# Attention decode with SwiGLU: the last V in W_Q's place, the first K ahead of the FFN weights, and spin matmuls in each pass

## The chip, the cores and the metric

One NeuronCore of a Trainium2 chip runs the kernel. The metric is the device time of one execution in microseconds (us). Engine names are those of the profile: PE is TensorE's matmul, PEld its weight load, DVE is VectorE, ACT ScalarE, POOL GpSimd, SP SyncE; SPq is SP's queue of DMA issues.

## What is computed

A decode step for four sequences. The input is normalised once, and the result is the input plus attention plus a gated FFN:

```python
xn = layernorm(x)                                    # x: (4, 1, 512)
q  = (xn @ wq)                                       # 32 heads of 128
k, v = the last 4096 of 16384 cached positions       # 8 K/V heads, each for 4 query heads
p  = softmax(q k^T / sqrt(128))
A  = (p v) @ wo
F  = (silu(xn @ w_gate) * (xn @ w_up)) @ w_down      # 512 -> 1792 -> 512
out = x + A + F
```

All of it is bf16. One K/V head with its four query heads is a group; K and V of a group are 4 MiB each for the four sequences. With eight groups, W_Q and W_O (4 MiB each) and three FFN matrices (1.75 MiB each), 81.0 MB come from HBM once each.

## The kernel before

**Tiles.** The 128 partitions hold 32 stretches of the window for each of the four sequences; a group's K and V are then 128 tiles of 128 x 128 (`KB` and `VB`, one buffer each, K loaded in two halves). A K tile is transposed on PE against the identity into PSUM (`transposes`, L371; eight tiles are a chunk, and three banks `ps_kt` take turns). A chunk is copied to SBUF (`KT`) by DVE (L301) or, for the five chunks of `ACT_CH`, by ACT (L250). `scores` (L384) multiplies the copied tile, as the stationary operand, by the 16 query columns of the group; a sequence's partitions thus also hold scores for the other sequences' queries.

**Softmax.** DVE takes maxima of the scores (L306, L308), PE transposes them (`maxima`, L391), and DVE builds from them a matrix of 16 x 16 (`CM`, L310 to L314) with which `shift` (L396, four matmuls of 512 columns) subtracts each query's maximum and masks the foreign sequences. ACT then takes the exponentials (L254) into `P`. `pv` has a matmul with ones for the denominators (L405) for every 16 tiles, and one matmul for each V tile (L407). `norm` on DVE (L318 to L325) divides and places the result for W_O.

**The order on PE.** The program begins with the Q projection (L351, 128 matmuls), then gate and up of the FFN (L358, 112 matmuls). Then a hardware loop of nine passes follows: pass r does transposes and scores of group r, then `pv` of group r - 1 (48 tiles, `maxima` of group r, the other 80), then `shift` of group r. `If` leaves out what a pass doesn't have: pass 0 has no `pv`, and pass 8 has only `down` (the FFN's last product, L417 and L421) and the last `pv`. Behind the loop a small permutation (L452) and the product with W_O (L460) add to the sum that `down` started in PSUM, and DVE and ACT copy the two halves of the result out.

**The order on DVE and ACT.** Before their loops, ACT computes the exponential of the FFN's gate (L246), and DVE finishes the gated product (L286 to L292), which `down` needs. Then come the groups, with `norm(r - 1)` behind `group(r)`.

**The order of the loads.** All large loads are issued by SP in one list: W_Q, gate, up, K0 (two halves), down, four of the 32 row blocks of W_O; then for each g from 1 to 7 the halves of K(g) and V(g - 1); then the last V in two halves, and the rest of W_O in two parts. A half of K waits until the same half of the group before is transposed (L210), V until `pv` of the group before is done (L215):

```python
def load_v(g):
    if g > 0:
        eng.wait_ge(s_pv, g + 1)
```

A wait in this list holds all that stands behind it.

Of the kernel before, what the change touches and what calls it, by code (L numbers as in the profile page):

```python
# [3 lines left out]
BF16 = mybir.dt.bfloat16  # L4
FP32 = mybir.dt.float32
ALU = mybir.AluOpType
# [4 lines left out]
def bass_parallel_sum__sliding_block_cached__swiglu_ffn__decode_kernel(  # L11
# [113 lines left out]
    d_v = sem("d_v")  # L125
    d_vh = sem("d_vh")
    s_const = sem("s_const")
# [36 lines left out]
    with nc.Block() as block:  # L164
# [39 lines left out]
        @block.sync  # L204
        def _(eng):
            H = NT // 2

            def load_k(g, h):
                if g > 0:
                    eng.wait_ge(s_tr, NCH * (g - 1) + (h + 1) * NCH // 2)  # L210
                eng.dma_start(KB[:, h * H:(h + 1) * H, :], kv_ap(A_k_cache, g, h * H, (h + 1) * H)).then_inc(d_k[h], 16)

            def load_v(g):
                if g > 0:
                    eng.wait_ge(s_pv, g + 1)  # L215
                for a, b, d in ((0, H, d_vh), (H, NT, d_v)) if g == HKV - 1 else ((0, NT, d_v),):
                    eng.dma_start(VB[:, a:b, :], kv_ap(A_v_cache, g, a, b)).then_inc(d, 16)  # L217
# [4 lines left out]
            eng.dma_start(WQ[:], wq_ap).then_inc(d_wq, 16)  # L222
# [12 lines left out]
            load_wo(2, WOB, NR)  # L235
            eng.wait_ge(s_y[0], 1)
            eng.dma_start(out_ap[0], y[0:B, :]).then_inc(d_out, 16)
            eng.wait_ge(d_out, 32)

        @block.scalar  # L240
        def _(eng):
            eng.dma_start(X[:], x_ap).then_inc(d_x, 16)
            eng.wait_ge(s_var, 1)
            eng.activation(st_std[:], st_var[:], ACT.Sqrt).then_inc(s_std, 1)
            eng.wait_ge(s_gu, 1)
            eng.activation(ex[:], gate_ps.rearrange("p (t b) -> p t b", b=B), ACT.Exp, scale=-1.0).then_inc(s_ex, 1)  # L246
            with eng.Fori(0, HKV) as r:
                for n, c in enumerate(ACT_CH):
                    eng.wait_ge(s_tr, r * NCH + (c + 1))
                    eng.activation(KT[:, c % 4], kt_ps[c % 3], ACT.Copy).then_inc(s_ea, 1)  # L250
                eng.wait_ge(s_pv, r + 1)
                for q in range(NB):
                    eng.wait_ge(s_mk, r * NB + (q + 1))
                    eng.activation(P[:, BT * q:BT * (q + 1), :], ps_S[q][:].rearrange("p (t n) -> p t n", n=NH),  # L254
                                   ACT.Exp, scale=SCALE).then_inc(s_p, 1)
            eng.wait_ge(s_acc, 1)
            eng.activation(y[64:64 + B, :], acc_ps[64:64 + B, 0:D // 2], ACT.Copy).then_inc(s_y[1], 1)  # L257
# [4 lines left out]
        def _(eng):  # L262
# [21 lines left out]
                            q_ps.rearrange("p (k h b) -> p k b h", k=HKV, b=B))  # L284
            eng.wait_ge(s_ex, 1)
            eng.tensor_scalar(ex[:], ex[:], 1.0, None, ALU.add)  # L286
            eng.drain()
            eng.reciprocal(ex[:], ex[:])
            eng.drain()
            eng.tensor_tensor(gs[:], gate_ps.rearrange("p (t b) -> p t b", b=B), ex[:], ALU.mult)  # L290
            eng.drain()
            eng.tensor_tensor(guT[:], up_ps.rearrange("p (t b) -> p t b", b=B), gs[:], ALU.mult).then_inc(s_guT, 1)  # L292

# [33 lines left out]

            group(0)
            with eng.Fori(1, HKV) as r:
                group(r)  # L330
                norm(r - 1)
# [7 lines left out]
        def _(eng):  # L339
# [13 lines left out]
            last.then_inc(s_q, 1)  # L353
            for w, d, o in ((WG, d_wg, gate_ps), (WU, d_wu, up_ps)):
                eng.wait_ge(d, 16)
                for t in range(NF):
                    for c in range(NC):
                        last = mm(o[:, t * B:(t + 1) * B],  # L358
                                  w[:].rearrange("p c (m t) -> p c t m", t=NF)[:, c, t, :], XnT[:, c, :],
                                  start=(w is WG and t == 0 and c == 0), stop=(c == NC - 1),  # L360
                                  skip_group_check=True)
            last.then_inc(s_gu, 1)
            eng.sem_inc(s_pv, 1)
# [35 lines left out]

            def pv(r, a, b):  # L400
                n = NT // DT
                for t in range(a, b):
                    if t % (NT // n) == 0:
                        e = t // (NT // n)
                        mm(den_ps, ones[:], P[:, DT * e:DT * (e + 1), :].rearrange("p t n -> p (t n)"),  # L405
                           start=(e == 0), stop=(e == n - 1), skip_group_check=True)
                    last = mm(O_ps, VB[:, t, :], P[:, t, :], start=False, stop=(t == NT - 1), skip_group_check=True)  # L407
                if b == NT:
                    last.then_inc(s_pv, 1)

            HD = D // 2
# [11 lines left out]

            with eng.Fori(0, HKV + 1) as r:
                with eng.If(r < HKV):
                    for c in range(NCH):
                        transposes(r, c)
                        if c >= 2:
                            scores(r, c - 2)
                    scores(r, NCH - 2)  # L430
                    scores(r, NCH - 1)
                with eng.If(r > HKV - 1):
                    down()
                    eng.wait_ge(d_vh, 16)
                with eng.If(r > 0):
                    eng.wait_ge(s_p, r * NB + NB)
                    eng.wait_ge(s_nrm, r)
                    with eng.If(r < HKV):
                        eng.wait_ge(d_v, r * 16)
                    pv(r, 0, 48)  # L440
                with eng.If(r < HKV):
                    maxima(r)
                with eng.If(r > 0):
                    pv(r, 48, NT // 2)
                    eng.wait_ge(d_v, r * 16)
                    pv(r, NT // 2, NT)
                with eng.If(r < HKV):
                    shift(r)

            eng.wait_ge(s_nrm, HKV + 1)  # L450
            for b in range(B):
# [3 lines left out]
            for q in range(3):  # L455
                eng.wait_ge(d_wo[q], 16)
                a, b = ((0, WOA), (WOA, WOB), (WOB, NR))[q]
                for e in range(a, b):
# [32 lines left out]
```

## Time and profile before

| | |
|---|---|
| time, median of 3 runs | 217.65 us (215.77 to 217.68) |
| the profiled execution: time, span | 217.74 us, 216.0 us |
| mean granted clock of PE | 0.826 |
| PE, PEld, DVE, ACT busy | 169.5, 147.8, 102.1, 60.8 us |
| HBM read, mean over the span | 81.01 MB, 375 GB/s |
| chain that ended last | DMA 60%, PE 31%, issue 4%, DVE 2% |

The span runs from the first to the last instruction of the profiled execution. The busy times are sums over the whole run; PE's includes the latency of each pipelined matmul, so it is not a measure of how full PE is. The chain is followed back from the last instruction to whatever released each step, so it tells which resource was waited for. The slices divide the span in forty equal parts of 5.4 us; `PEclk` in them is the clock granted to PE, in tenths of full speed, and a 5 is half clock.

### The profile page before, as it was taken

How to read it: one execution, taken by the hardware profiler on the slowest of the kernel's cores; microseconds unless marked ns; L12 is line 12 of the kernel's file. 1: busy time of each engine (PE TensorE's matmuls, PEld its weight loads, DVE VectorE, ACT ScalarE, POOL GpSimd, SP SyncE). 2: the span in 40 equal slices, each digit the busy share in tenths (PEclk: the TensorE clock that was granted, in tenths of full speed). 3: DMA queues.
4: the chain of work that ended last, by engine and by line, in shares of the span. 5: the costliest groups of instructions: out<-in, count | busy, mean ns of one | idle time of the engine just before them, and what ended most of it. 6: DMA issues, size and time to landing. Idle time of an engine off the chain costs nothing.

```text
span 216.0 us, 8057 instructions
## 1 busy us (share of the span) xinstructions
PE 169.5 (78%) x3520; PEld 147.8 (68%) x3520; DVE 102.1 (47%) x209; ACT 60.8 (28%) x77; POOL 5.8 (3%) x29
## 2 busy tenths in 40 slices
PE   0157689519979995998899699979959997974655
PEld 0157689508977994797779679977958896634533
DVE  5200058703863882388258636854961685300200
ACT  2200014205522550345055215605430551210000
POOL 8200000000000000000000000000000000000000
PEclk9999999955985997699679958997995899566557
DMA  7999999999898899999999999998999993099930
GB/s 280 400 416 431 427 421 393 394 473 397 326 394 303 349 419 434 394 397 428 422 413 479 391 434 437 434 431 367 425 407 431 455 407 152 12 425 419 454 150 1
DMA packets 4639, 81.12 MB, mean 376 GB/s; under 512 B 524, under 2 KB 536, under 8 KB 792
## 3 DMA queue, kind: packets, MB, share of 16 engines
q1 hardware_dynamic: 4616, 81.01, 89.3%
q8 instruction: 6, 0.10, 0.2%
q10 hardware_dynamic: 16, 0.01, 0.0%
q14 instruction: 1, 0.01, 0.0%
HBM read 81.01 MB, written 0.00 MB: 375 GB/s over the span
## 4 chain that ended last, share of the span: by engine, by line
DMA 60%; PE 31%; issue 4%; DVE 2%; SPq 1%; DVEq 0%
DMA vbuf<-in_A_v_cache_dram 39%; DMA kbuf<-in_A_k_cache_dram 12%; PE ps_o L407 11%; DMA wo_sb<-in_A_wo_dram 9%; PE ps_kt L371 8%; PE ps_o L405 6%; PE ps_kt L460 3%; PE ps_s L384 2%; DVE kT L301 1%; PE ps_s L396 1%; PE ps_kt L391 1%; DVE mx L306 1%; SPq L217 1%; SPq L224 0%; DVE y_sb L336 0%
## 5 line engine op out<-in xcount | busy, mean ns | idle before, releaser
L371 PE MATMUL ps_kt<-ident,kbuf 128*128 128x128 bf16 x1024 | 80.3, 227 | 1.3 <-DMA kbuf<-in_A_k_cache_dram 1.3
L371 PEld LDWEIGHTS ps_kt<-ident,kbuf 128*128 128x128 bf16 x1024 | 63.7, 102 | 4.9 <-issue 3.2
L301 DVE COPY kT<-ps_kt 128x1024 bf16<-128x1024 bf16 x88 | 57.5, 685 | 19.0 <-PE ps_kt L371 18.7
L250 ACT ACTIVATE kT<-ps_kt 128x1024 bf16<-128x1024 bf16 x40 | 41.0, 1024 | 35.4 <-PE ps_kt L371 35.4
L384 PE MATMUL ps_s<-qC,kT 128*128 128x16 bf16 x1024 | 44.9, 170 | 2.6 <-DVE kT L301 1.9
L384 PEld LDWEIGHTS ps_s<-qC,kT 128*128 128x128 bf16 x1024 | 37.4, 97 | 4.4 <-DVE kT L301 4.1
L407 PEld LDWEIGHTS ps_o<-p,vbuf 128*128 128x128 bf16 x1024 | 36.8, 105 | 3.2
L407 PE MATMUL ps_o<-p,vbuf 128*128 128x16 bf16 x1024 | 38.4, 175 | 0.0
L254 ACT ACTIVATE p<-ps_s 128x512 bf16<-128x512 f32 x32 | 16.5, 602 | 69.9 <-PE ps_s L396 69.9
L405 PE MATMUL ps_o<-p,ones 128*128 128x256 bf16 x64 | 22.6, 354 | 14.4 <-DMA vbuf<-in_A_v_cache_dram 13.6
L306 DVE TENSOR_REDUCE mx<-ps_s 128x16 f32<-128x512 f32 x32 | 22.1, 692 | 6.7 <-PE ps_s L384 3.6
L396 PE MATMUL ps_s<-cm,own 128*128 128x512 bf16 x32 | 14.4, 606 | 5.4 <-issue 5.4
L405 PEld LDWEIGHTS ps_o<-p,ones 128*128 128x128 bf16 x64 | 6.5, 102 | 16.4 <-issue 14.0
L318 DVE TENSOR_REDUCE den<-ps_o 128x16 f32<-128x256 f32 x8 | 3.4, 425 | 30.2 <-PE ps_o L407 30.2
L310 DVE TENSOR_TENSOR junk<-ps_kt,moff 16x128 f32<-16x128 bf16 x8 | 2.2, 279 | 17.8 <-PE ps_kt L391 17.8
L396 PEld LDWEIGHTS ps_s<-cm,own 128*128 128x128 bf16 x32 | 3.5, 128 | 9.9 <-issue 9.9
L460 PE MATMUL ps_kt<-wo_sb,oP 128*4 128x256 bf16 x64 | 7.1, 414 | 2.7 <-DMA wo_sb<-in_A_wo_dram 2.2
L460 PEld LDWEIGHTS ps_kt<-wo_sb,oP 128*4 128x4 bf16 x64 | 3.8, 122 | 5.7 <-DMA wo_sb<-in_A_wo_dram 2.7
L351 PE MATMUL ps_s<-xnT,wq_sb 128*128 128x4 bf16 x128 | 3.6, 166 | 5.1 <-DMA wq_sb<-in_A_wq_dram 5.1
L257 ACT ACTIVATE y_sb<-ps_kt 4x256 bf16<-4x256 f32 x1 | 0.4, 375 | 24.2 <-PE ps_kt L460 24.2
L351 PEld LDWEIGHTS ps_s<-xnT,wq_sb 128*128 128x128 bf16 x128 | 3.5, 104 | 5.2 <-issue 5.2
L344 PE MATMUL ps_s<-i,xn 4*128 4x4 f32 x4 | 0.6, 261 | 7.4 <-POOLq L202 7.4
(63 smaller groups left out, 52.5 us busy)
## 6 DMA issues: line engine op xcount, KB each, us to landing
kbuf<-in_A_k_cache_dram SPq DMA_DIRECT2D x16, 2048.0 KB, 12.3
vbuf<-in_A_v_cache_dram SPq DMA_DIRECT2D x7, 4096.0 KB, 14.2
wq_sb<-in_A_wq_dram SPq DMA_DIRECT2D x1, 4096.0 KB, 12.2
vbuf<-in_A_v_cache_dram SPq DMA_DIRECT2D x2, 2048.0 KB, 9.7
wo_sb<-in_A_wo_dram SPq DMA_DIRECT2D x1, 3328.0 KB, 19.3
wg_sb<-in_B_w_gate_dram SPq DMA_DIRECT2D x1, 1792.0 KB, 16.0
wu_sb<-in_B_w_up_dram SPq DMA_DIRECT2D x1, 1792.0 KB, 21.3
wd_sb<-in_B_w_down_dram SPq DMA_DIRECT2D x1, 1792.0 KB, 33.5
```

Source lines behind the costliest of these rows:

```text
L250: eng.activation(KT[:, c % 4], kt_ps[c % 3], ACT.Copy).then_inc(s_ea, 1)
L254: eng.activation(P[:, BT * q:BT * (q + 1), :], ps_S[q][:].rearrange("p (t n) -> p t n", n=NH), ACT.Exp, scale=SCALE).then_inc(s_p, 1)
L301: eng.tensor_copy(KT[:, c % 4], kt_ps[c % 3]).then_inc(s_ev, 1)
L306: eng.tensor_reduce(mx[:, q, :], ps_S[q][:].rearrange("p (t n) -> p n t", n=NH), AX.X, ALU.max)
L318: eng.tensor_reduce(den[:], den_ps.rearrange("p (t n) -> p n t", n=NH), AX.X, ALU.add)
L351: last = mm(q_ps[:, h * B:(h + 1) * B], WQ[:, c, h * Dh:(h + 1) * Dh], XnT[:, c, :], start=(c == 0 and h == 0), stop=(c == NC - 1), skip_g ...
L371: last = eng.transpose(kt_ps[c % 3][:, k, :], KB[:, CH * c + k, :], ident[:])
L384: last = mm(ps_S[q][:, NH * t:NH * (t + 1)], KT[:, c % 4, k, :], QC[:], start=(t == 0), stop=False, skip_group_check=True)
L396: mm(ps_S[q][:].rearrange("p (t n) -> p t n", n=NH), own[:], CM[:].unsqueeze(1).to_broadcast([128, BT, NH]), start=False, stop=True, skip_ ...
L405: mm(den_ps, ones[:], P[:, DT * e:DT * (e + 1), :].rearrange("p t n -> p (t n)"), start=(e == 0), stop=(e == n - 1), skip_group_check=True)
L407: last = mm(O_ps, VB[:, t, :], P[:, t, :], start=False, stop=(t == NT - 1), skip_group_check=True)
L460: last = mm(acc_ps[64 * n:64 * n + B, 0:HD], OP[:, e, :], WO[:, e, HD * n:HD * (n + 1)], start=False, stop=(e == NR - 1), skip_group_check ...
```

## The change

- **The last V.** The 4 MiB of W_Q are needed for the Q projection alone. The last V gets that place (`VL`, of which `WQ` is now a view), so its load waits only for the Q projection (`s_q`). It is in two halves with a semaphore each. `down` and the `pv` of the last group stand behind the loop on PE, which has eight passes.
- **The first loads.** K0 goes ahead of gate and up. The whole of W_O is loaded behind the last V, in parts of 16, 14 and 2 row blocks.
- **The FFN.** Gate and up are multiplied inside pass 0, behind `maxima`. ACT's exponential for it stands behind group 0's exponentials, and DVE's part behind `group(0)`.
- **Spin matmuls.** `spin` multiplies the matrix of ones by 512 columns into a bank `ps_kt` that is free at that point; nothing reads the result. A pass has three ahead of `maxima`, three behind it, and one inside `pv`; `pv` is no longer cut at 48 tiles for `maxima`.
- **Copies.** `ACT_CH` changes from (2, 5, 9, 11, 13) to (3, 5, 8, 10, 13).

```diff
-    ACT_CH = (2, 5, 9, 11, 13)
+    ACT_CH = (3, 5, 8, 10, 13)
-    WOA = 4
-    WOB = 30
+    WOS = (16, 30)
...
-    WQ = sb("wq_sb", [128, NC, HQ * Dh], BF16, 512)
+    VL = sb("vlast", [128, NT, Dh], BF16, 512)
+    WQ = VL[:].rearrange("p t d -> p (t d)").rearrange("p (c n) -> p c n", c=NC)
...
# SP
+            load_k(0, 0)
+            load_k(0, 1)
             eng.dma_start(WG[:], wg_ap).then_inc(d_wg, 16)
             eng.dma_start(WU[:], wu_ap).then_inc(d_wu, 16)
-            load_k(0, 0)
-            load_k(0, 1)
             eng.dma_start(WD[:], wd_ap).then_inc(d_wd, 16)
-            load_wo(0, 0, WOA)
             for g in range(1, HKV):
                 load_k(g, 0)
                 load_k(g, 1)
                 load_v(g - 1)
-            load_v(HKV - 1)
-            load_wo(1, WOA, WOB)
-            load_wo(2, WOB, NR)
+            eng.wait_ge(s_q, 1)
+            for h in range(2):
+                eng.dma_start(VL[:, h * H:(h + 1) * H, :], kv_ap(A_v_cache, HKV - 1, h * H, (h + 1) * H)).then_inc(d_vl[h], 16)
+            load_wo(0, 0, WOS[0])
+            load_wo(1, WOS[0], WOS[1])
+            load_wo(2, WOS[1], NR)
...
# ACT
-            eng.wait_ge(s_gu, 1)
-            eng.activation(ex[:], gate_ps..., ACT.Exp, scale=-1.0).then_inc(s_ex, 1)
-            with eng.Fori(0, HKV) as r:
+            group(0)
+            eng.wait_ge(s_gu, 1)
+            eng.activation(ex[:], gate_ps..., ACT.Exp, scale=-1.0).then_inc(s_ex, 1)
+            with eng.Fori(1, HKV) as r:
+                group(r)
...
# PE
+                    if t == NT * 3 // 8:
+                        spin(1)
...
+            def spin(n):
+                for _ in range(n):
+                    mm(ps_kt[2][:], ones[:], own[:].unsqueeze(1).to_broadcast([128, 4, 128]),
+                       skip_group_check=True)
...
+            with eng.Fori(0, HKV) as r:
+                for c in range(NCH):
+                    transposes(r, c)
+                    if c >= 2:
+                        scores(r, c - 2)
+                scores(r, NCH - 2)
+                scores(r, NCH - 1)
+                spin(3)
+                maxima(r)
+                spin(3)
+                with eng.If(r < 1):
+                    gate_up()
+                with eng.If(r > 0):
+                    eng.wait_ge(s_nrm, r)
+                    eng.wait_ge(d_v, r * 16)
+                    pv(VB, 0, NT)
+                shift(r)
+
+            down()
+            eng.wait_ge(s_p, HKV * NB + NB)
+            eng.wait_ge(s_nrm, HKV)
+            eng.wait_ge(d_vl[0], 16)
+            pv(VL, 0, NT // 2)
+            eng.wait_ge(d_vl[1], 16)
+            pv(VL, NT // 2, NT)
```

`gate_up` holds the loop that stood in front of PE's loop before, unchanged.

More of the change, by code (lines that the diff above doesn't have):

```diff
@@ L125, in bass_parallel_sum__sliding_block_cached__swiglu_ffn__decode_kernel @@
     d_v = sem("d_v")
-    d_vh = sem("d_vh")
+    d_vl = [sem("d_vl%d" % h) for h in range(2)]
     s_const = sem("s_const")
@@ L244, in _, with group @@
             eng.activation(st_std[:], st_var[:], ACT.Sqrt).then_inc(s_std, 1)
-            eng.wait_ge(s_gu, 1)
-            eng.activation(ex[:], gate_ps.rearrange("p (t b) -> p t b", b=B), ACT.Exp, scale=-1.0).then_inc(s_ex, 1)
-            with eng.Fori(0, HKV) as r:
+            def group(r):
                 for n, c in enumerate(ACT_CH):
@@ L328, in _ @@
             group(0)
+            eng.wait_ge(s_ex, 1)
+            eng.tensor_scalar(ex[:], ex[:], 1.0, None, ALU.add)
+            eng.drain()
+            eng.reciprocal(ex[:], ex[:])
+            eng.drain()
+            eng.tensor_tensor(gs[:], gate_ps.rearrange("p (t b) -> p t b", b=B), ex[:], ALU.mult)
+            eng.drain()
+            eng.tensor_tensor(guT[:], up_ps.rearrange("p (t b) -> p t b", b=B), gs[:], ALU.mult).then_inc(s_guT, 1)
             with eng.Fori(1, HKV) as r:
@@ L353, in _ @@
             last.then_inc(s_q, 1)
[L354 to L362, printed above, removed]
             eng.sem_inc(s_pv, 1)
@@ L398, in shift, with pv @@
                        start=False, stop=True, skip_group_check=True).then_inc(s_mk, 1)
-            def pv(r, a, b):
+            def pv(V, a, b):
                 n = NT // DT
```

49 lines of the change are left out of this document (15 added, 34 removed).

## The prediction

> **What bounds the kernel now.** The slices come first, because 81 MB pass through: is the DMA ever idle, and what does PE's clock do meanwhile?
>
> ```profile
> PEclk9999999955985997699679958997995899566557
> DMA  7999999999898899999999999998999993099930
> GB/s 280 400 416 431 427 421 393 394 473 397 326 394 303 349 419 434 394 397 428 422 413 479 391 434 437 434 431 367 425 407 431 455 407 152 12 425 419 454 150 1
> q8 instruction: 6, 0.10, 0.2%
> ```
>
> The DMA is full except at the ends, thin in slices 10 to 13, and empty in slice 34. PE's clock sags once per pass. The chain in order of time says why the hole is there:
>
> ```profile
> 62.32 0.78 issue
> ...
> 68.60 15.01 DMA vbuf<-in_A_v_cache_dram
> ...
> 168.07 13.48 DMA vbuf<-in_A_v_cache_dram
> ...
> 187.17 0.54 SPq L217
> ...
> 188.39 19.31 DMA wo_sb<-in_A_wo_dram
> 207.75 6.08 PE ps_kt L460 x56
> 213.85 0.41 DVE y_sb L336
> ```
>
> V of group 6 lands at 168.07 + 13.48 = 181.55. V of group 7 is issued at 187.17, when `pv` has left the one V buffer; W_O queues behind it, so 56 of its matmuls run after 207.75. The stages in between:
>
> ```profile
> 13.00:28.00 15.00, 10.67 (x242) 10.46 (x243) 1.20 (x4) 0.22 (x1) 0.00 (x0) 1.00 1.01 429
> ...
> 62.30:69.00 6.70, 5.92 (x140) 4.99 (x140) 2.12 (x6) 0.00 (x0) 0.00 (x0) 0.58 0.85 340
> 69.00:83.00 14.00, 12.04 (x260) 10.91 (x257) 10.78 (x21) 7.18 (x9) 0.00 (x0) 0.96 0.93 376
> ...
> 181.50:187.20 5.70, 5.39 (x138) 4.76 (x139) 0.98 (x5) 0.00 (x0) 0.00 (x0) 0.62 0.00 0
> ```
>
> The columns are length, busy time of PE, PEld, DVE, ACT, POOL, then PE's clock, DMA share, GB/s. Fed without a break the DMA moves about 430 GB/s (429 in the first row): 8.39 MB of K and V take 19.5 us, and from V1's landing (68.60 + 15.01 = 83.61) to V6's five passes take 97.94, 19.59 each. Those passes are DMA-bound. From 62 to 83 it is PE that issues V1 late. But PE is only just off the bound:
>
> ```profile
> 108.45 1.87 PE L396 MATMUL ps_s<-cm,own 128*128 128x512 bf16 x4
> ...
> 110.11 2.03 PE L371 MATMUL ps_kt<-ident,kbuf 128*128 128x128 bf16 x24
> ...
> 121.42 0.36 PE L384 MATMUL ps_s<-qC,kT 128*128 128x16 bf16 x8 [0.24 <-DVE kT L301]
> ...
> 122.57 0.26 DVE L308 TENSOR_REDUCE m<-mx 128x16 bf16<-128x64 f32 x1
> 123.12 0.28 PE L405 MATMUL ps_o<-p,ones 128*128 128x256 bf16 x1 [1.35 <-DMA vbuf<-in_A_v_cache_dram]
> ...
> 123.65 0.27 PE L405 MATMUL ps_o<-p,ones 128*128 128x256 bf16 x1
> ```
>
> PE waits 1.35 us for V and then has no slack to show: `shift` 1.66, transposes and scores 110.11 to 121.78 = 11.67. A PV block (one L405, sixteen L407) costs 0.53 at full clock (123.12 to 123.65), eight of them 4.2. All of PV(6), mostly at half clock and with the maximum's transpose inside, took the time from V6's landing to V7's issue, 5.6 with 0.3 of issue.
>
> **The change, term by term.** The sum is made against this execution: span 216.0, its time 217.74, so 1.74 lie around it. The median of the runs, 217.65, is 0.09 below, and nothing is corrected for that.
>
> *The first pass.* K0 moves ahead of 3.67 MB of gate and up. Terms:
>
> ```profile
> 13.17 3.55 PE L351 MATMUL ps_s<-xnT,wq_sb 128*128 128x4 bf16 x128 [5.10 <-DMA wq_sb<-in_A_wq_dram]
> 17.31 3.52 PE L358 MATMUL ps_o<-xnT,wg_sb 128*128 128x4 bf16 x56 [0.59 <-DMA wg_sb<-in_B_w_gate_dram]
> 27.92 2.74 PE L371 MATMUL ps_kt<-ident,kbuf 128*128 128x128 bf16 x24 [1.33 <-DMA kbuf<-in_A_k_cache_dram]
> ...
> 42.25 0.22 PE L391 MATMUL ps_kt<-ident,m 128*16 128x128 bf16 x1 [1.12 <-DVE m L308]
> 47.85 1.89 PE L396 MATMUL ps_s<-cm,own 128*128 128x512 bf16 x4 [5.38 <-issue]
> ```
>
> W_Q landed at 13.2; half of K0 (2.10 MB) follows 4.9 later, at 18.1, after the Q matmuls end (16.72). Pass 0 starts 9.8 us earlier, and its maximum's transpose comes at 42.25 - 9.8 = 32.45. Three spins run ahead of it under the wait for DVE; 0.25 for it and three spins behind make 33.3. Gate and up, 2 x 3.52, land before they are needed and end at 40.4. Now `pv` is skipped, as before, when PE stood 5.38 us for "issue" ahead of `shift`. That is code that is not there yet, and the new skip is as long (136 matmuls with their weight loads). Bounds: 0, if gate and up give the code time to come, and 5.4; I take 2.7. `shift` starts at 43.1 rather than 47.85: 4.7 earlier, between 7.4 and 2.0.
>
> Given back in pass 1: the exponential and four vector operations of the FFN now stand behind pass 0's exponentials and ahead of DVE's copies; PE gets three transposed chunks ahead, then waits for those copies. Between 0 and three late copies (2.1, a copy's 0.69 being shown below) I take 1.0. The wait for the maximum, formerly under PV, is exposed: last score to m16 1.05 (121.78 to 122.83), transpose 0.25, three spins 0.65, so 1.95 instead of 0.78 of issue (the chain's first row): 1.2. The spin in PV, for the transpose that leaves it, costs up to 0.2. So V1 is issued at 68.60 - 4.7 + 1.0 + 1.2 + 0.1 = 66.2, and lands after 15.0 like before, at 81.2 (78.5 to 83.9).
>
> The 0.52 MB of W_O that leaves the front of the queue (1.2 us) adds nothing here: V1 waits for PE, not for bytes. K1 and K2 are released by transposes that come earlier than before; the SP queue passes them in the old order. The other split of the copies (still five on ACT, eleven on DVE) costs nothing:
>
> ```profile
> L301 DVE COPY kT<-ps_kt 128x1024 bf16<-128x1024 bf16 x88 | 57.5, 685 | 19.0 <-PE ps_kt L371 18.7
> ```
>
> DVE's copies fill 7.2 us of a pass and wait for PE; without that cover a late copy would cost 0.69 a pass.
>
> *Steady passes.* A spin has no row. The nearest is the 512-column `shift`: 0.43 us each in the row above at half clock, 0.23 by halving. What PE's pass becomes hangs on the clock. Two windows of 3.41 us at half clock, one that stayed (124.84 to 128.26), one at whose end it rose (145.32 to 148.74), by form:
>
> ```profile
> L407 PE MATMUL ps_o<-p,vbuf 128*128 128x16 bf16 x80 | 3.1, 177 | 0.0
> L405 PE MATMUL ps_o<-p,ones 128*128 128x256 bf16 x5 | 1.9, 378 | 0.0
> L396 PE MATMUL ps_s<-cm,own 128*128 128x512 bf16 x1 | 0.6, 587 | 0.0
> ```
>
> ```profile
> L407 PE MATMUL ps_o<-p,vbuf 128*128 128x16 bf16 x58 | 2.3, 176 | 0.0
> L396 PE MATMUL ps_s<-cm,own 128*128 128x512 bf16 x4 | 1.7, 581 | 0.0
> L405 PE MATMUL ps_o<-p,ones 128*128 128x256 bf16 x3 | 1.1, 374 | 0.0
> ```
>
> ```profile
> 141.91:145.32 3.41, 2.73 (x83) 1.00 1.03 442
> 145.32:148.74 3.42, 3.42 (x65) 0.50 1.04 446
> 148.74:152.15 3.41, 3.41 (x73) 1.00 0.87 332
> ```
>
> Counted in moving columns, 3,072 did not raise the clock and 3,744 did. A window wholly in the new PV holds 3.2 / 0.53 blocks of 512 columns and a spin: 3,600. With six spins ahead and no pause it lies nearer the upper row, so I take the clock as held in most passes and lost in those where PE waits for V. Held, PE's pass is PV 4.5 (eight blocks and a spin), `shift` 0.95, transposes and scores 11.1 (the first 24 transposes in 1.4 instead of 2.03), tail 1.95: 18.5, under 19.5. Lost: 5.5 (a spin of 0.43 for the transpose) + 1.66 + 11.67 + 1.95 = 20.8, over it. Up to half of the passes may be of the second kind before the DMA ceases to set the pace, and a late PE does not wait, which favours the first kind. So 19.59 stays, and V6 lands at 81.2 + 97.9 = 179.1.
>
> [...]
>
> *The last V and the tail.* V7's two halves go to W_Q's place straight behind V6 (`s_q` is long past), W_O behind them. The hole of 5.7 us and more closes: 8.39 MB after V6 end 19.5 later, at 198.6. PE's path from V6's landing becomes the longer one. Its rows at half clock:
>
> ```profile
> 188.79 1.02 PE L417 MATMUL ps_kt<-xf,i 4*4 4x256 f32 x4
> 189.74 3.15 PE L421 MATMUL ps_kt<-wd_sb,guT 128*4 128x256 bf16 x28
> ...
> 202.38 0.43 DVE L318 TENSOR_REDUCE den<-ps_o 128x16 f32<-128x256 f32 x1 [13.79 <-PE ps_o L407]
> ...
> 204.56 1.02 PE L460 MATMUL ps_kt<-wo_sb,oP 128*4 128x256 bf16 x8 [0.54 <-DVE oP L334]
> ```
>
> Issue 0.3; PV(6) 4.4 to 5.5, I take 4.8; `shift` 0.95 to 1.7, 1.2; `down` 2.05 to 4.1, 2.6 (dense work in front of it); PV(7), whose halves are there, 4.8 again; normalisation to W_O 202.2 to 204.56, 2.4; 64 W_O matmuls at 0.108 (6.08 / 56) or half of that, 3.5 to 6.9, 5.9, since the pause in front cools PE; copy and output 213.85 to 216.0, 2.15. Together 24.2, between 22.1 (the DMA's 19.5, four matmuls, the end) and 28.5. PV(7) and `down` become straight code behind the loop: fetched in order, under 0.3 for the branch that goes. Span 179.1 + 24.2 = 203.3; time **205.0 us**.
>
> **Rivals.**
> - *All goes well:* no code wait, clock held. V1 78.5, V6 176.4, the tail at the DMA's bound 22.1: span 198.5, time 200.2. For it: 3,600 columns are near 3,744. Against: every idle wait for V so far dropped the clock.
> - *The clock falls in every PV:* PE sets a pass of 20.8. PV(0) starts at 61.0, PV(6) at 185.8; the tail at half clock 28.5: span 214.3, time 216.0, no change to tell. For it: 3,600 is not 3,744.
> - *Slower: the spins run at half clock too.* Seven more matmuls on PE's path, and PE the bound: pass 1.3 + 0.25 + 1.3 + 5.5 + 1.66 + 11.67 = 21.7, and 22.0 with a cold start of the transposes. PV(6) at 193, span 221.5, time 223. It loses from a pass of 21.1. For it: the scores' thin end and DVE's 1.05 stand in one window with them. Against: the transposes just ahead ran at full clock (the row from 148.74, and most slices).
> - *Code fetched anew.* The loop on PE grows from 854 to 1,032 instructions, two for each matmul of a pass. If it outgrew its store, one wait of 5.4 per pass would make 205 + 7 x 5.4 = 243. Against: six fetches for eight passes in the page's q8 row, so the old loop stayed resident. [...]
>
> **How the numbers follow.** Forecast 0.64, all well 0.20, clock lost 0.10, spins cold 0.04, refetch 0.02. A measurement of this kernel tells about 1%, 2.2 us. Faster: 0.64 + 0.20 + half of 0.10 = 0.89; same 0.05; slower 0.06. The range: from just under the good case to where most passes lose the clock, 199.0 to 212.5; outside lie most of the third rival, the last two, and a little of the best case.
>
> **What would show it.** After V6 the DMA stays full, and V7 is issued some 10 us before V6 lands; W_O's last wait is PE's, not the DMA's. V1 issued near 66; an "issue" wait ahead of the first `shift` under 5.4. PEclk at 9 in most slices from 60 on; V landings 19.6 apart. Landings over 20.3 apart, with PE never waiting for V, would refute the steady term; a DMA with a hole after V6 the largest one.

## The result and the profile after

The changed kernel takes **204.4 us** (median of 4 runs, 203.2 to 205.2), the kernel before on the same chip 217.7 (215.8 to 220.4): a ratio of 0.941, 95% interval 0.933 to 0.950. The profiled execution took 203.2 with a span of 201.4. Ratios are formed over undisturbed executions alone, beside the kernel before on the same chip, which took some 213 us on the chip of the fifth to the eighth experiment, so medians in us are given as well.

The first view is the page's slices, to be laid beside those of before:

```profile
span 201.4 us, 8063 instructions
PEclk9999999658699999999999999999999999999959
DMA  6999999999889599999999999999999999999990
GB/s 222 462 404 423 427 433 424 428 452 423 347 345 397 195 469 417 417 469 417 417 423 443 436 404 430 443 443 397 433 465 430 404 439 452 417 423 436 416 391 7
q8 instruction: 7, 0.11, 0.2%
```

Four things stand out. The hole in slices 33 and 34 is gone. PE's clock, which sagged once per pass, stays at 9 from slice 11 to slice 37. It falls in slices 7 to 10, which begin with the FFN's matmuls in their new place. And the thin stretch around slices 10 to 13 is still there, with a slice of 195 GB/s in it. The 9 of the first slices is not to be trusted, before or after: the first 24 transposes, at 17.99, take 2.74 us, and 24 of them take 1.50 later, at full clock. The chain in order of time (start, length, what) shows what sets the end now:

```profile
17.99 2.74 PE ps_kt L370 x24
...
33.92 6.66 PE ps_o L417 x112
40.59 2.55 issue
...
43.83 1.28 ACT L255
...
49.01 0.70 DVE kT L301
...
162.58 0.54 SPq L217
...
165.08 32.11 DMA wo_sb<-in_A_wo_dram
197.23 1.93 PE ps_kt L476 x32
199.19 0.41 DVE y_sb L344
```

Before, the chain ended with a V that was issued at 187.17 and a W_O that landed at 207.75. Now V7 and W_O are issued straight behind V6, from 163.16 on, and the last of W_O lands at 197.23. In between the chain goes from pass to pass through PE and DVE, not through a V. The stretches from one issue of V to the next (columns as before: length, busy PE, PEld, DVE, ACT, POOL, clock, DMA share, GB/s) give the rate:

```profile
67.32:86.38 19.06, 17.65 (x405) 15.56 (x404) 11.95 (x24) 7.18 (x9) 0.00 (x0) 1.00 0.92 388
86.38:105.38 19.00, 17.64 (x405) 15.56 (x404) 11.96 (x24) 7.18 (x9) 0.00 (x0) 1.00 1.02 438
...
124.37:143.36 18.99, 17.65 (x405) 15.55 (x404) 11.95 (x24) 7.18 (x9) 0.00 (x0) 1.00 1.00 429
143.36:162.58 19.22, 17.81 (x405) 15.48 (x404) 11.95 (x24) 7.18 (x9) 0.00 (x0) 1.00 1.01 435
```

Full clock in every pass, and 19.0 us per pass. A pass uses 8.39 MB, that is 441 GB/s, while the DMA delivers 423 (the row left out) to 438. PE can run that much faster than the DMA only because it began with a lead: in the first of these passes the DMA still had slack (388 GB/s at a share of 0.92), so its data were early. The lead is used up in pass 6, in PE's timeline of the tail:

```profile
177.49 0.27 PE L404 MATMUL ps_o<-p,ones 128*128 128x256 bf16 x1 [0.27 <-DMA vbuf<-in_A_v_cache_dram]
...
182.77 0.60 PE L434 MATMUL ps_kt<-xf,i 4*4 4x256 f32 x4
183.30 1.69 PE L438 MATMUL ps_kt<-wd_sb,guT 128*4 128x256 bf16 x28
184.92 0.28 PE L404 MATMUL ps_o<-p,ones 128*128 128x256 bf16 x1
...
190.80 0.29 PE L468 MATMUL ps_kt<-dr,oT 128*128 128x32 bf16 x4 [1.40 <-DVE oT L325]
193.09 3.58 PE L476 MATMUL ps_kt<-wo_sb,oP 128*4 128x256 bf16 x32 [2.00 <-DMA wo_sb<-in_A_wo_dram]
197.23 1.91 PE L476 MATMUL ps_kt<-wo_sb,oP 128*4 128x256 bf16 x32 [0.57 <-DMA wo_sb<-in_A_wo_dram]
```

The 0.27 ahead of the first line is the only wait for V in the whole kernel. V6 landed at 177.2, and behind it PE runs at full clock until 190.4, when it waits for DVE's `norm`; then it waits for W_O, 2.57 us in two waits. So the tail belongs to the DMA.

### The profile page after: what moved, and what is told of

Its sections match the earlier page's. It is cut to its first block, busy times and chain, and to the rows that moved or that the text cites. A ratio compares the mean times of both kernels' runs of the same rounds, so it can differ in the third digit from the quotient of the medians.

```text
span 201.4 us, 8063 instructions
## 1 busy us (share of the span) xinstructions
PE 166.0 (82%) x3576; PEld 144.6 (72%) x3576; DVE 102.4 (51%) x209; ACT 60.7 (30%) x77; POOL 5.8 (3%) x29
## 3 DMA queue, kind: packets, MB, share of 16 engines
q1 hardware_dynamic: 4616, 81.01, 94.8%
HBM read 81.01 MB, written 0.00 MB: 402 GB/s over the span
## 4 chain that ended last, share of the span: by engine, by line
PE 51%; DMA 24%; DVE 13%; issue 6%; ACT 1%; SPq 1%; DVEq 1%; ACTq 0%
PE ps_kt L370 20%; DMA wo_sb<-in_A_wo_dram 16%; PE ps_s L383 10%; PE ps_o L406 9%; DMA kbuf<-in_A_k_cache_dram 8%; DVE kT L301 6%; PE ps_kt L425 3%; PE ps_o L417 3%; PE ps_o L404 3%; DVE mx L306 3%; DVE den L318 1%; PE ps_kt L476 1%; DVE m L308 1%; ACT p L255 1%; PE ps_kt L390 1%
## 5 line engine op out<-in xcount | busy, mean ns | idle before, releaser
L370 PE MATMUL ps_kt<-ident,kbuf 128*128 128x128 bf16 x1024 | 79.5, 226 | 1.7 <-DMA kbuf<-in_A_k_cache_dram 1.2
L370 PEld LDWEIGHTS ps_kt<-ident,kbuf 128*128 128x128 bf16 x1024 | 62.5, 101 | 3.8 <-DMA kbuf<-in_A_k_cache_dram 1.3
L406 PEld LDWEIGHTS ps_o<-p,vbuf 128*128 128x128 bf16 x896 | 28.8, 96 | 2.1
L406 PE MATMUL ps_o<-p,vbuf 128*128 128x16 bf16 x896 | 30.0, 169 | 0.0
L404 PE MATMUL ps_o<-p,ones 128*128 128x256 bf16 x64 | 17.3, 270 | 0.3 <-DMA vbuf<-in_A_v_cache_dram 0.3
L425 PE MATMUL ps_kt<-own,ones 128*128 128x512 bf16 x56 | 16.0, 379 | 0.0
L395 PE MATMUL ps_s<-cm,own 128*128 128x512 bf16 x32 | 9.1, 409 | 2.5 <-issue 2.5
L359 PE MATMUL ps_s<-xnT,vlast 128*128 128x4 bf16 x128 | 3.6, 166 | 5.2 <-DMA vlast<-in_A_wq_dram 5.2
L476 PE MATMUL ps_kt<-wo_sb,oP 128*4 128x256 bf16 x64 | 5.5, 343 | 2.6 <-DMA wo_sb<-in_A_wo_dram 2.6
L359 PEld LDWEIGHTS ps_s<-xnT,vlast 128*128 128x128 bf16 x128 | 3.5, 104 | 5.3 <-issue 5.3
```

Source lines behind the costliest of these rows:

```text
L359: last = mm(q_ps[:, h * B:(h + 1) * B], WQ[:, c, h * Dh:(h + 1) * Dh], XnT[:, c, :], start=(c == 0 and h == 0), stop=(c == NC - 1), skip_g ...
L370: last = eng.transpose(kt_ps[c % 3][:, k, :], KB[:, CH * c + k, :], ident[:])
L395: mm(ps_S[q][:].rearrange("p (t n) -> p t n", n=NH), own[:], CM[:].unsqueeze(1).to_broadcast([128, BT, NH]), start=False, stop=True, skip_ ...
L406: last = mm(O_ps, V[:, t, :], P[:, t, :], start=False, stop=(t == NT - 1), skip_group_check=True)
L425: mm(ps_kt[2][:], ones[:], own[:].unsqueeze(1).to_broadcast([128, 4, 128]), skip_group_check=True)
L476: last = mm(acc_ps[64 * n:64 * n + B, 0:HD], OP[:, e, :], WO[:, e, HD * n:HD * (n + 1)], start=False, stop=(e == NR - 1), skip_group_check ...
```

## The experiments

The theory: closing the hole and holding the clock each bring their part, the DMA paces the middle, and the first K ahead of the FFN weights brings some 2.4 us at V1. Twelve kernels were run, four on one chip each time, with the kernel before beside them; the changed kernel itself was not run again there.

**Without spins.** All seven spin matmuls are taken out of the changed kernel.

```diff
-                spin(3)
                 maxima(r)
-                spin(3)
...
-                    if t == NT * 3 // 8:
-                        spin(1)
```

> The changed kernel without its seven spins per pass; nothing else differs. Theory (the spins hold PE's clock, and PE's pass of 19.0 us is what paces the changed kernel): the clock falls in every PV as it did before; a pass is then PV 5.1, shift 1.66, transposes and scores 11.7, the exposed maximum 1.3, in all 19.8 instead of 19.0, so V6 lands some 4 us later, and the tail runs partly at half clock, 2 to 6 us more: 209 to 213 us. Rival (the loads set the pace, the spins only fill time in which PE would wait): within 1 us of 204.4, or a little faster.

Measured: 208.7 us (207.5 to 209.8), ratio 0.967 [0.959, 0.975], span 205.8, clock 0.842 against 0.949. The passes from the first to the last, beside the DMA share and rate:

```profile
67.79:87.22 19.43, 17.66 (x398) 15.69 (x397) 11.95 (x24) 7.18 (x9) 0.00 (x0) 0.85 0.94 398
...
146.72:166.86 20.14, 18.42 (x398) 16.67 (x397) 12.14 (x24) 7.18 (x9) 0.00 (x0) 0.84 0.99 419
```

A pass without spins has less work and takes longer, 19.4 to 20.1 instead of 19.0, as the theory had it; the time lies just under its range. The spins are worth 4.3 us by the medians, 5.6 by the ratios, once the hole is closed.

**One V buffer again.** V7 waits for `pv` of group 6, as before; all else stays.

```diff
-            eng.wait_ge(s_q, 1)
+            eng.wait_ge(s_pv, HKV)
...
-                eng.dma_start(VL[:, h * H:(h + 1) * H, :], ...
+                eng.dma_start(VB[:, h * H:(h + 1) * H, :], ...
```

> The changed kernel with the last V back in the one V buffer: its load waits for PV of group 6, and all of W_O stands behind it. Theory: PV(6) ends near 181.8, so V7 is issued there instead of at 163; the 8.39 MB of V7 and W_O then need 19.5 us from some 183.3, W_O lands near 204 instead of 197, and the time is 210 to 213 us, the DMA empty for about 6 us. Rival (W_O behind the last V, not the place of V, is what shortens the tail, and PE's clock the rest): less than 3 us slower, under 207.5.

Measured: 212.2 us (211.9 to 214.6), 0.981 [0.974, 0.988]; the profiled execution was the longest, span 212.8. V7 issues at 183.45, and the hole is back:

```profile
PEclk9999999558899999999999999999999999995555
GB/s 259 431 403 428 430 429 428 422 453 440 149 425 296 388 400 413 474 394 431 428 416 450 403 431 453 419 419 462 425 406 431 462 443 123 55 443 434 422 227 1
```

Slices 33 and 34 carry 123 and 55 GB/s, W_O lands at 207.05, and the tail runs at half clock (the last four slices are at 5). The time is in the range of the theory. The other place for V7 is worth 7.8 us by medians, 8.7 by ratios.

**The FFN weights first.** Loads, FFN matmuls and FFN vector work go back ahead of pass 0; spins and V7's place stay.

```diff
-            load_k(0, 0)
-            load_k(0, 1)
             eng.dma_start(WG[:], wg_ap).then_inc(d_wg, 16)
             eng.dma_start(WU[:], wu_ap).then_inc(d_wu, 16)
+            load_k(0, 0)
+            load_k(0, 1)
...
-                with eng.If(r < 1):
-                    gate_up()
```

> The changed kernel with gate and up loaded and multiplied ahead of the first K again, as before; the rest as changed. Theory (V1 is issued when PE has done PV(0), and the first K in front lets PE start 9.8 us earlier but gives 6.7 back to gate and up and 2.4 to DVE's FFN work): V1 is issued 0 to 3 us later than at 67.3, and 0.3 to 0.7 of that reaches the end: 204 to 207 us. Rival (the order of the first loads is a main part of the gain): 208 us or more.

Measured: **201.3 us** (200.2 to 202.4), 0.931 [0.923, 0.940], span 199.6: neither expectation. The slices and two passes:

```profile
PEclk9999999999999999999999999999999999999959
...
GB/s 237 433 412 431 427 427 409 336 365 453 422 401 440 466 420 397 424 460 427 417 427 456 420 407 450 430 420 420 447 447 417 417 453 433 410 430 437 423 306 4
```

```profile
63.49:82.83 19.34, 17.80 (x405) 15.49 (x404) 11.95 (x24) 7.18 (x9) 0.00 (x0) 1.00 1.01 430
...
140.99:160.42 19.43, 17.80 (x405) 15.48 (x404) 11.95 (x24) 7.19 (x9) 0.00 (x0) 1.00 1.00 432
```

V1 is issued at 63.49 instead of 67.32, the thin stretch is one slice pair (336 and 365), and from the first passes on the clock doesn't fall before the end. The first row has the DMA full at once; a pass is then 19.4, its own pace. So in the traces K0 ahead, with the FFN's matmuls and vector work behind it, costs the changed kernel time; which of the three costs how much, this run can't tell. Of the parts of the change it is the one that did not help. By the medians the kernel is 3.1 us quicker than the changed one, but on another chip; by the ratios it is one point, and their intervals overlap, so the size of the gain is not shown.

**V7's place alone**, put on the kernel before: the loop ends one pass earlier and PV(7) stands behind it; no spins, FFN weights first.

```diff
-    WQ = sb("wq_sb", [128, NC, HQ * Dh], BF16, 512)
+    VL = sb("vlast", [128, NT, Dh], BF16, 512)
+    WQ = VL[:].rearrange("p t d -> p (t d)").rearrange("p (c n) -> p c n", c=NC)
...
-            load_v(HKV - 1)
+            eng.wait_ge(s_q, 1)
+            for h in range(2):
+                eng.dma_start(VL[:, h * H:(h + 1) * H, :], ...
```

> The kernel before with one part of the change: the last V in W_Q's place, its PV behind the loop. Order of the first loads, FFN, split of W_O, no spins: as before. Theory: V6 lands near 181.5 as before, but V7 and W_O are there some 19 us later; PE at half clock sets the tail with 28.5 us, span 209 to 210, time 210 to 212.5 us: about half of the 13.3 us. Rival (the hole is all): the DMA sets the tail, 203.5 span, 205 to 206 us.

Measured: 207.1 us (205.2 to 208.4), 0.951 [0.942, 0.960], span 206.4; the medians on this chip give 8.7 us, the ratio 10.6. The result lies between the two expectations, nearer the rival. The hole is gone, and the end is PE's, at half clock:

```profile
198.49 5.65 PE L459 MATMUL ps_kt<-wo_sb,oP 128*4 128x256 bf16 x56 [3.81 <-DMA wo_sb<-in_A_wo_dram]
```

W_O is there at 198.49, 1.3 later than in the changed kernel, but 56 matmuls remain and take 5.65 (0.101 each) where the last 32 took 1.91 (0.060 each). This part alone brings most of the gain.

**Spins alone**, on the kernel before: six behind the scores, one in `pv`.

```diff
                     scores(r, NCH - 1)
+                    spin(6)
...
+                    spin(1)
                     pv(r, 48, NT // 2)
```

> The kernel before with the seven spins alone: six behind the scores, one inside PV; the last V, the loads, FFN and W_O as before. Theory (the spins hold the clock, and the loads pace the passes once PE is at full clock): V1 is issued 1 to 3 us earlier than at 68.6, the passes stay 19.4 to 19.6 apart, the hole after V6 stays (PV(6) shorter by 0.9), the tail with W_O gains little: 213 to 216 us, 0 to 1.5% faster. Rival (the spins are the main part): 210 us or less.

Measured: 215.2 us (212.3 to 217.7; ten runs), 1.003 [0.996, 1.010]. In the profile of its shortest run V6 is issued 3.9 us earlier than before (164.21 for 168.07), but the hole remains:

```profile
183.47 0.54 SPq L217
...
184.69 19.11 DMA wo_sb<-in_A_wo_dram
203.85 4.54 PE ps_kt L467 x54
```

V7 leaves at 183.47, when PV(6) ends, and all W_O stands behind it. Alone the spins bring nothing that can be told, within the theory's range; with the hole closed they bring 4 to 6. The two parts of the gain don't add. A gain of a per cent or two under the open hole is not excluded: the kernel with one V buffer has the spins too, beside other parts of the change, and a ratio of 0.981.

**No spin in PV**, only the six at the maximum:

```diff
-                    if t == NT * 3 // 8:
-                        spin(1)
```

> The changed kernel without the one spin inside PV; the six around the maximum stay. Theory (what counts is the moving columns in a window of 3.41 us): a window wholly in PV now holds some 3,300 columns instead of 3,600; the clock falls in part of the passes, PEclk shows 5 to 8 in some slices, and the time is 205 to 207.5 us. Rival (the six spins ahead of PV are enough): within 0.5 us of the changed kernel, at a clock of 0.94 or more.

Measured: 204.2 us (203.8 to 205.6), 0.959 [0.950, 0.968]; span 202.0, clock 0.949. The clock held in every pass, as the rows of two show:

```profile
87.12:105.91 18.79, 17.44 (x404) 15.46 (x403) 11.94 (x24) 7.18 (x9) 0.00 (x0) 1.00 1.01 432
...
144.03:163.43 19.40, 17.59 (x404) 15.38 (x403) 11.95 (x24) 7.18 (x9) 0.00 (x0) 1.00 1.00 432
```

The early passes are 0.2 shorter, by one spin; the last two are 19.4, since PE has caught up with the DMA. The spin in PV isn't needed, and taking it away gains nothing either.

**A hundred small matmuls ahead of the Q matmuls**, 4 columns each, so that all of PE's code lies 200 instructions further on:

```diff
             eng.wait_ge(s_xnT, 1)
+            for _ in range(100):
+                mm(ps_kt[2][:, 0:4], ones[:], own[:, 0:4], skip_group_check=True)
```

> The changed kernel with 100 small matmuls (4 columns, result unread) on PE while it waits for W_Q, so that all code behind them stands 200 instructions later. Theory (the 2.55 us of issue ahead of the first shift are a block of code that is asked for too late, and where a block begins decides): the wait ahead of the first shift changes by over 1.5 us, most likely to under 1; V1 is issued 2 us earlier, and 1 to 2 us of it reach the end: 202.5 to 203.5. Rival (the wait belongs to the jump itself): still 2.5 us or more there, the time unchanged within 0.5.

Measured: 205.5 us (205.4 to 207.3), 0.966 [0.956, 0.975], span 203.7. The wait ahead of the first `shift` did not go but grew:

```profile
45.33 1.89 PE L397 MATMUL ps_s<-cm,own 128*128 128x512 bf16 x4 [3.71 <-issue]
```

The change that the theory expected, of over 1.5 us, did not come. But the 1.16 can't be put down to the new place either. In two kernels PE's code is as long as in the changed one and stands at the same place, and their waits are 3.44 (one V buffer) and 3.95 (the next experiment) where the changed kernel has 2.55. So something other than the place moves the length by 1.4 us, and what it is stays open.

**The FFN's vector work later, and the table early.** Gate and up are copied away by ACT, DVE's four operations go behind pass 1's copies, and a small exponential loads ACT's table while nobody waits:

```diff
+            eng.activation(warm[:], st_var[:], ACT.Exp)
...
             group(0)
-            eng.wait_ge(s_ex, 1)
-            eng.tensor_scalar(ex[:], ex[:], 1.0, None, ALU.add)
...
+            group(1)
+            eng.wait_ge(s_ex, 1)
+            eng.tensor_scalar(ex[:], ex[:], 1.0, None, ALU.add)
...
+            norm(0)
```

> The changed kernel with the FFN off the way of pass 1: ACT copies gate and up out of PSUM behind its exponential, DVE's four FFN operations stand behind group 1's work, and ACT touches the exponential once at the start, so that the 1.28 us of table load ahead of the first exponentials go. Theory (PE's wait of 2.39 us for DVE in pass 1 is the FFN and the table in front of the copies): the wait shrinks to under 0.8, V1 is issued 1.5 to 2 us earlier, 1 to 2 us reach the end: 202.5 to 203.5. Rival (PE is held by something else there, or the loads swallow it): within 0.5 us of 204.4.

Measured: 201.9 us (200.6 to 204.7), 0.945 [0.930, 0.960], span 199.2. V1 leaves at 64.77 rather than 67.32, although this run has a longer code wait:

```profile
44.19 1.89 PE L403 MATMUL ps_s<-cm,own 128*128 128x512 bf16 x4 [3.95 <-issue]
```

The wait of the first scores for DVE is no longer among the waits. From `shift` to V1's issue it is 20.6 us instead of 24.2, so DVE's and ACT's work on the FFN cost up to 3.6 us there, more than was expected; the table and DVE's operations were not moved apart. The time is 2.5 us lower by the medians, which the ratio, from another chip, doesn't bear out. On its own chip the kernel is 2.4 us quicker by the medians than the changed kernel without the spin in PV.

**The first of W_O early**, on the kernel with the FFN weights first: eight of the W_O rows go ahead of K1 to fill the thin stretch.

```diff
-    WOS = (16, 30)
+    WOS = (8, 30)
...
             eng.dma_start(WD[:], wd_ap).then_inc(d_wd, 16)
+            load_wo(0, 0, WOS[0])
```

> The kernel with the FFN first again (e3), and 8 of the 32 row blocks of W_O (1.05 MB) loaded behind the FFN's last weights, ahead of K1. Theory (in e3 the loads set the pace from the first V on, and what is left is the thin stretch from 34 to 46 us, some 2.3 us of transfer, in which K1 waits for PE): W_O's part fills it and is missing at the end; 199 to 200.3 us. Rival (it pushes K1 and V0 back by what it fills): 201 to 202 us, like e3.

Measured: 202.5 us (200.2 to 204.8), 0.932 [0.923, 0.940]: no gain. The stretch is filled, and the last W_O came 1.2 earlier, at 194.27 instead of 195.46, but 48 matmuls then remain, at half clock:

```profile
164.48 29.74 DMA wo_sb<-in_A_wo_dram
...
194.27 5.25 PE ps_kt L474 x48
```

5.25 us (0.109 each) instead of 1.91 for 32 (0.060 each). In this execution (203.5 us, span 201.7) the half-clock tail took back more than the DMA gave, and V1 left 2.3 later than in the kernel with the FFN weights first (65.80 for 63.49); its clock had fallen near 42.7 (the three spins at 41.57 take 0.81, the three at 43.04 take 1.46). It is one of the two longer executions of the four; what kept the other two, 200.2 and 201.4, from gaining is not shown.

**Twice the spins**, six and six and two in PV:

```diff
-                spin(3)
+                spin(6)
                 maxima(r)
-                spin(3)
+                spin(6)
...
-                        spin(1)
+                        spin(2)
```

> The changed kernel with 14 spins per pass: six ahead of the maximum, six behind, two inside PV. Theory (PE paces the changed kernel): each spin past the wait for DVE costs 0.22 us, a pass grows from 19.0 to some 20.3, V6 lands 7 to 8 us later and the time is 209 to 213 us. Rival (PE has slack against the loads): under 207 us.

Measured: 208.9 us (208.3 to 209.8), 0.970 [0.964, 0.975], span 208.0. A pass is now wholly PE's:

```profile
109.53:129.50 19.97, 19.08 (x412) 16.24 (x411) 11.96 (x24) 7.18 (x9) 0.00 (x0) 1.00 0.98 411
```

Seven more spins cost 1.0 per pass, 0.14 each, less than the 0.2 of the one in PV: those in front of the maximum's transpose first fill the wait for DVE, 0.45 a pass. The pass goes from 19.0 to 20.0 (20.3 was expected), and in this row the DMA falls to a share of 0.98. So what is added to PE past that wait makes the pass longer, while what is taken away soon meets the DMA, as the kernel without the PV spin showed.

**Three spins**, only those in front of the transpose:

```diff
                 spin(3)
                 maxima(r)
-                spin(3)
...
-                        spin(1)
```

> The changed kernel with three spins per pass, those ahead of the maximum, which run while PE would wait for DVE. Theory (moving columns in a window): PV alone holds 3,070 columns in 3.41 us, the clock falls in it, and the time is 206.5 to 209, as without spins. Rival (the pause ahead of PV is what lets the clock fall, and three spins fill it): clock 0.93 or more, PE's pass 18.3, the time 202.5 to 204.5 us.

Measured: 206.6 us (206.2 to 207.7), 0.959 [0.954, 0.965], span 205.2, clock 0.858:

```profile
PEclk9999995558699999589958999999699669966958
```

The clock falls in five of the six passes from V1 on, near 83, 103, 144, 161 and 181 us: to fill the wait is not enough, the three behind it count. PV is the same as in the kernel without the spin in PV, so they are what tells the two apart. No long pause goes ahead of the fall: PE was busy for 18.45 of the 19.5 us of the pass from 87.31, its waits there were 0.24, 0.46 and 0.28, and the clock fell behind them, in PV: a matmul with ones takes 0.27 up to 102.29 and 0.37 from 102.81 on.

**Pass 0 written out.** The first pass is straight code ahead of the loop, with the FFN matmuls in their place; nothing is skipped any more.

```diff
+            front(0)
+            gate_up()
+            shift(0)
-            with eng.Fori(0, HKV) as r:
+            with eng.Fori(1, HKV) as r:
...
-                with eng.If(r < 1):
-                    gate_up()
-                with eng.If(r > 0):
```

> The changed kernel with pass 0 written out ahead of PE's loop, so that no code is skipped in it; the same work in the same order. Theory (the 2.6 to 4 us of issue ahead of the first shift are the skip of PV's code): no wait of over 0.5 us there, V1 issued 2 to 3 us earlier than at 67.3, 202 to 203 us. Rival (the code of the next stretch comes late whether skipped or not): the wait stays at 2 us or more, the time within 0.7 of 204.4.

Measured: 202.7 us (202.2 to 203.5), 0.941 [0.935, 0.947], span 200.6. PE's timeline around the first `shift`:

```profile
36.91 3.50 PE L417 MATMUL ps_o<-xnT,wu_sb 128*128 128x4 bf16 x56
40.27 1.87 PE L395 MATMUL ps_s<-cm,own 128*128 128x512 bf16 x4
...
46.88 0.38 PE L383 MATMUL ps_s<-qC,kT 128*128 128x16 bf16 x8 [2.80 <-DVE kT L301]
...
56.95 0.44 PE L370 MATMUL ps_kt<-ident,kbuf 128*128 128x128 bf16 x5 [1.16 <-issue]
```

No wait: `shift` follows gate and up at once, 2.9 earlier than in the changed kernel. Where nothing is skipped the code wait is gone, so it belongs to the skip of `pv`. More than that no run shows: that PE waits there for code was an estimate, and the profile calls the wait issue. Part of it comes back as waiting for DVE (2.80 instead of 2.39) and as 1.16 of issue late in the loop's first pass, at 56.95, so V1 gains 1.7 (65.62). By the median the kernel is 1.7 quicker than the changed one, by the ratio, from another chip, the same; a gain in time is not shown.

## Why the prediction came right, and where its steps did not

**The time** was 205.0 against 204.4; in the profiled execution the span was 203.3 against 201.4. The 1.9 between them are three errors: V1 was issued 1.1 later than said, the five passes took 95.3 instead of 97.9, and the way from V6's issue to its landing was 0.4 shorter (14.6 for 15.0). The tail came out to the tenth, by luck.

**The first pass** held step by step: start 17.99 (18.1), the maximum's transpose 32.95 (32.45), gate and up done at 40.59 (40.4), the code wait 2.55 (2.7), `shift` at 43.13 (43.1). For the code wait that was luck: 2.7 was only the middle between 0 and 5.4, and the two kernels with the same code on PE had 3.44 and 3.95.

**Wrong: what DVE gives back in pass 1.** I took 1.0 for it, between 0 and 2.1. The timeline of all engines after the first `shift`, of the changed kernel:

```profile
43.83 1.28 ACT L255 ACT_TABLE_LOAD   x1 [13.99 <-PE ps_s L395]
...
47.33 0.19 DVE L330 TENSOR_SCALAR ex<-ex 128x56 f32<-128x56 f32 x1 [13.19 <-ACT ex L260]
...
49.76 0.36 PE L383 MATMUL ps_s<-qC,kT 128*128 128x16 bf16 x8 [2.39 <-DVE kT L301]
```

PE waited 2.39, above my upper end. The bound had the exponential and DVE's four operations in it, but not the 1.28 us in which ACT loads its table for the exponential. In the kernel before, that load came with the first exponential of the FFN, at 5.73, ahead of pass 0, where nobody waited for it; with the FFN behind pass 0 it stands ahead of pass 0's exponentials. With the load early and the FFN operations later, both at once, the wait is gone and V1 is 2.6 earlier.

**Wrong: the first K ahead as a gain.** I credited the earlier first `shift` with 4.7, and V1 with 2.4. The kernel with the FFN weights first has its `shift` at 44.39, only 1.26 later than the changed one, and 3.5 ahead of the kernel before, in the same order of loads: those 3.5 are its shorter code wait (1.88 for 5.38). Of the changed kernel's own 4.7, too, 2.8 are the code wait (2.55 for 5.38). And from `shift` to V1's issue the kernel with the FFN weights first takes 19.1 where the changed kernel takes 24.2, since its clock doesn't fall there and no FFN work stands in pass 1. In the changed kernel the clock falls in the midst of gate and up, at 36.8, while PE is busy without a break:

```profile
36.00:37.00 1.00, 1.00 (x20) 1.00 (x19) 0.00 (x0) 0.00 (x0) 0.00 (x0) 0.88 1.07 459
37.00:38.00 1.00, 1.00 (x20) 1.00 (x19) 0.00 (x0) 0.00 (x0) 0.00 (x0) 0.50 1.07 459
```

In the kernel with pass 0 written out it falls there as well: the three spins in front of them, at 32.93, take 0.82, full clock, and the `shift` behind them, at 40.27, takes 1.87, half clock, with no wait in front. So the fall comes under the FFN's matmuls of 4 columns, ahead of any code wait, and pass 1 begins with a PE at half clock. The sum had no term for that: it took over pass 1 from the kernel before, where the clock was down as well. So the step that failed is the comparison: I held the code wait and the order of loads together, gave to the second what came with the first, and did not ask what the FFN's matmuls do where they now stand. The order of the loads alone was not run. The kernel with the FFN's vector work later still has K0 first, and at 201.9 it is close to the 201.3 here, so the order itself need not be what costs.

**Wrong in kind, small in size: the steady passes.** I had them bound by the DMA at 19.59 and PE's pass at 18.5. PE's pass is 19.0, and PE sets it. One pass of the changed kernel, PE first and then DVE:

```profile
105.21 1.03 PE L395 MATMUL ps_s<-cm,own 128*128 128x512 bf16 x4
106.07 1.50 PE L370 MATMUL ps_kt<-ident,kbuf 128*128 128x128 bf16 x24
108.13 0.36 PE L383 MATMUL ps_s<-qC,kT 128*128 128x16 bf16 x8 [0.56 <-DVE kT L301]
...
119.06 0.22 PE L390 MATMUL ps_kt<-ident,m 128*16 128x128 bf16 x1 [0.45 <-DVE m L308]
```

```profile
105.39 0.42 DVE L318 TENSOR_REDUCE den<-ps_o 128x16 f32<-128x256 f32 x1 [4.14 <-PE ps_o L406]
...
107.38 1.89 DVE L301 COPY kT<-ps_kt 128x1024 bf16<-128x1024 bf16 x3
```

With the clock held, PE's three chunks of transposes are done in 1.5 us, but DVE's `norm` of the group before stands in front of the copies and ends only at 107.38, so the scores wait 0.56; I had called the copies free, covered by PE. The rest nearly cancels: the end of the pass took 2.07 for my 1.95, PV 4.3 (119.87 to 124.20) for 4.5. The DMA's own pace is 19.4 (the kernel with the FFN weights first), so the value I took for it was 0.2 high.

**Right: the clock.** It rises at 53.8 and holds to 190.4. I had it lost in up to half of the passes; none of those behind 53.8 is lost. My window argument, that 3,600 columns in PV lie near enough to 3,744, was not what decided: without the spin in PV the clock holds as well (1.00 in the five passes from 68.28 on), and with that same PV and three spins it falls (0.84 to 0.94 in the five from 67.87). With none it falls too (0.84 and 0.85). The length of 3.41 us is that of the shortest stretch at half clock in the two traces (145.32 to 148.74 before, 50.4 to 53.8 after); the others are 6.8, 10.2 and 17.1 long. The lower of my two windows was also counted short: it held the maximum's transpose besides, which makes 3,200 columns and not 3,072.

**Right: code resident.** The q8 row shows 7 packets (0.11 MB) where the old loop had 6 (0.10): the loop of 1,032 instructions ran its eight passes on 7 in all. So the longer loop stayed resident, and the rival that fetched it in every pass is out. The row shows 8 with 200 instructions more, and 9 with pass 0 written out. At what length a loop would be fetched anew no run shows.

**Two errors in the tail that met.** I had 24.2 behind V6, set by PE, and 22.1 as the DMA's bound. It was 24.2, and the DMA's: V6 at 177.2, W_O there at 197.23 (20.0 for 8.39 MB, not 19.5), then 32 matmuls of the second half (1.9) and 2.2 to the end. My floor had four matmuls there, those of the last W_O piece; in fact the second piece of 14 rows comes together with it, and 32 wait. PE's path was too long: its clock stayed up, so PV(6), `shift`, `down`, PV(7) took 4.5, 0.9, 2.2 and 4.4, and PE came to W_O 2.0 us before the data.

**The hole** closed as said; it was the largest term of the sum. V7 went out 14 us ahead of V6's landing, rather than some 10.

## What to carry to other kernels

First close the DMA's holes, then look at the engines: the spins alone brought nothing that could be told while a hole of some 6 us waited at the end, and they were worth 4 to 6 us once it had gone. When work is moved, list what it has carried along silently (an exp table load, a vector operation at the head of a queue, a skip of code, small matmuls under which the clock fell), since these cost here as much as the move promised. And check each part of a change by undoing it: K0 ahead of the FFN went in with two good parts, and without it V1 left 3.8 us earlier.

## What the runs showed of the hardware that I had not expected

- Skipping a block of code in the first pass cost PE between 1.2 us of "issue" (the first of W_O early) and 5.5 (V7's place alone), with nearly the same number of matmuls skipped; written out as straight code the wait there was zero, with 1.16 later. What sets its length is open: with the same code on PE it was 2.55, 3.44 and 3.95.
- With six 512-column matmuls at the end of the scores and one in PV the clock stayed at full speed for 136 us (53.8 to 190.4), and with the six alone in all five passes that were measured, 68.28 to 163.43; with three it fell in five of six passes, though PE was busy for 89.93 of the 98.39 us of the first five. Under matmuls of 4 columns it fell with PE busy for the whole 3 us before, at 36.8 in the changed kernel.
- The DMA moved 423 to 438 GB/s per pass in the steady state, and 427 to 433 in five passes of the kernel with the FFN weights first. 81.01 MB take 188 us at 431. The quickest kernel's span of 199.6 lies 12 above it, 4.1 of them behind the last W_O.
